# Which engine joins the weight words and subtracts the low parts: attention and two expert layers on one Trainium2 core

## The chip, the cores and the metric

The kernel runs on one core of a Trainium2 chip. Its engines are PE (TensorE, matmuls), DVE (VectorE), ACT (ScalarE), POOL (GpSimd) and SP (SyncE, which here only issues DMAs). Each works through its own list of instructions in order and waits on semaphores for the others. The metric is device microseconds (us) of one execution; lower is better.

## The reference, cut to what matters

```python
# attention with a decaying state; r, k, v, w: (2, 8, 768, 48), u: (8, 48)
for t in range(S):
    cur = einsum('bhd,bhe->bhde', u * k_t, v_t)
    y[:, :, t] = einsum('bhd,bhde->bhe', r_t, state + cur)
    state = w_t[..., None] * state + einsum('bhd,bhe->bhde', k_t, v_t)
x = y as (1536, 384)
h = x @ w_in                       # first layer, (384, 2048), weights in float64
x = (h * sigmoid(h)) @ w_out       # (2048, 384), weights in float64
e = argmax(x @ w_gate)             # second layer: one of 8 experts per token
out = gate_e * (relu(x @ w1[e]) @ w2[e])    # 384 -> 1024 -> 384
```

## The kernel before, in words

**Precision.** Every matmul operand is split in two float32r parts, a high part (a rounding copy on ACT) and a low part (operand minus high part). A product is three matmuls: high·high, high·low, low·high. So each weight piece, each activation tile and each attention output costs one copy and one subtraction on top of the matmuls.

**Weights of the first layer** arrive as float64 words in 16 pieces `rawd` of 128x768 words (`d_load`). A piece becomes float32 in place: `d_s` (lines 344, 345; 342 where the string `L3` says ACT) shifts the low 32-bit word's top three mantissa bits into place and fetches the sign, both on 16-bit quarter words; `d_abs` (349, ACT) rescales the high word; `d_or` (357, DVE) shifts the high word left by three and joins it with the low one. Then `d_h` (361, ACT) makes the high part in `wt` and `d_c` (369, POOL) the low part.

**Attention** takes 128 tokens of one batch per step, 12 steps (`at1` to `at8b`). DVE runs two scans (168, 180) over the decays `w`, multiplies `kh` (215) and, for steps 0, 1 and 2, `rh` (220; POOL from step 3 on). POOL multiplies `tk` (187, 188), DVE reduces it to `dg` (226, one number per head and token), and `at2b` writes `A`, eight 128x128 diagonal matrices with `dg` on the diagonal: ACT and POOL four each for steps 0 and 1 (232, 233), one POOL instruction of 128x1024 from step 2 on (235). DVE copies the masked scores over `A` (268), and PE multiplies.

**The first layer** works in units: 6 chunks of 256 tokens times 8 units of 256 features. `s1` (397) is 18 matmuls into the PSUM tile `s1`, of which there are two; ACT applies Silu twice, to `gh` (403, rounded) and to `sg` in SBUF (404); `s1b` (413) subtracts, `gl = sg - gh`, on DVE in even units and POOL in odd ones; `s2` (422) is 12 matmuls into `acc`. The PSUM tile is free again after the second Silu. Chunk 0 converts the 16 pieces as it goes (`tick`), and the tables `STAGES` and `AHEAD` say in which unit each part of an attention step is issued. After a chunk, `r1` to `r5` route its tokens: 16 products `jk` on DVE (459), some small operations, two indirect DMAs from POOL.

**The second layer** has 32 units of the same form, with Relu (407); its `gl` (415, DVE) reads the PSUM tile itself. The low parts of its weights are on DVE and POOL (384).

**Order.** The first instructions stand in an order written by hand (`manual_schedule`). The rest is ordered by a scheduler from the order of issue, priorities and its own picture of the times, separately for each engine, so an edit in one place can reorder others.

Of the kernel before, what the change touches and what calls it, by code (L numbers as in the profile page):

```python
# [8 lines left out]
F32 = mybir.dt.float32  # L9
# [26 lines left out]

# engine of the third limb subtraction of each weight piece: D = DVE, A = ACT
L3 = "DADADDDDAADDDDAA"
# MoE unit in which each stage of attention steps 2.. is issued
STAGES = (  # L40
# [10 lines left out]
)  # L51
# MoE unit before the loads of steps 3.. are issued
AHEAD = (0, 4, 9, 17, 24, 25, 44, 52, 60)


def bc(ap, shape):
    return ap.to_broadcast(shape)


def fast_path(ctx, tc, wp, rk, tk, vv, uu, ub, wd, wpc, wg, wgb, out, xs, flag):  # L60
# [161 lines left out]
    def at2b(n):  # L222
        d = st[n]
        dg = d["dg"] = wk.tile([128, 8], F32, name="dg")
        if n >= 2:
            nc.vector.tensor_reduce(dg.unsqueeze(2), d["tk"][:, 0].rearrange("p (h d) -> p h d", d=D), AX.X, ALU.add)
        else:
            nc.vector.tensor_copy(dg, d["dp"].rearrange("p a b -> p (a b)"))
        A = d["A"] = wk.tile([128, 8, 128], F32, name="A", bufs=2)
        if n < 2:  # L230
            for h in range(4, 8):
                nc.scalar.activation(out=A[:, h], in_=ident, func=AF.Copy, scale=dg[:, h:h + 1])
            nc.gpsimd.tensor_tensor(out=A[:, 0:4], in0=bc(ident.unsqueeze(1), [128, 4, 128]), in1=bc(dg[:, 0:4].unsqueeze(2), [128, 4, 128]), op=ALU.mult)
        else:
            nc.gpsimd.tensor_tensor(out=A, in0=bc(ident.unsqueeze(1), [128, 8, 128]), in1=bc(dg.unsqueeze(2), [128, 8, 128]), op=ALU.mult)

    def at_q2(n):
        nc.scalar.activation(out=jq, in_=st[n]["QF"], func=AF.Square, accum_out=q2[:, n:n + 1])

# [7 lines left out]
    def at3c(n):  # L247
        nc.scalar.copy(st[n]["Kt"], st[n]["kp"])
# [65 lines left out]
    def at8b(n):  # L314
# [23 lines left out]

    def d_s(m):
        h = dr[m].bitcast(U16).rearrange("p (n t) -> p n t", t=4)  # L340
        if L3[m] == 'A':
            nc.scalar.activation(out=h[:, :, 0], in_=h[:, :, 1], func=AF.Copy, scale=2.0 ** -13, bias=2.0 ** -14 - 0.5)  # L342
        else:
            nc.vector.tensor_scalar(h[:, :, 0], h[:, :, 1], 13, None, op0=ALU.logical_shift_right)  # L344
        nc.vector.tensor_scalar(h[:, :, 1], h[:, :, 3], 1 << 15, None, op0=ALU.bitwise_and)  # L345

    def d_abs(m):
        hi = words(m)[1].bitcast(F32)
        nc.scalar.activation(out=hi, in_=hi, func=AF.Abs, scale=2.0 ** -112)
# [17 lines left out]
    def d_c(m, eng):
        hi = words(m)[1].bitcast(F32)
        lz["pool"] = eng.tensor_tensor(out=wt[m][:, 1], in0=hi, in1=wt[m][:, 0].bitcast(F32), op=ALU.subtract)  # L369
        dr.pop(m)  # L370
# [14 lines left out]

    # ---------------- one pair of feature blocks
    PASS = ((0, 0), (0, 1), (1, 0))
    gt = {}

    def s1(u, w, x, moe1):  # L390
        s = ps.tile([128, 2, 256], F32, name="s1", bufs=2)
        wv = w.rearrange("p l (k f) -> p l k f", k=3)
        for fi in range(2):
            n = 0
            for a, b in PASS:
                for k in range(3):
# [802 lines left out]
```

## Time and profile before

| | us |
|---|---|
| three runs | 507.19, 509.21, 510.77 |
| median | 509.21 |
| profiled execution, first to last instruction | 509.3 |
| chunk 0's result is copied out (line 452, first time) | at 139.5 |
| first matmuls of the second layer | from about 359 |

The page gives no other time for the profiled execution than its span. In the rows below a busy time is the time in which an engine executes; a DVE instruction that has started and is held up counts as busy. `name L123` is the tile and the line. Names have no buffer numbers there.

### The profile page before, as it was taken

The page shows a single profiled execution, that of the slowest core. Times are in us where ns is not written, and L with a number is a line of the kernel's source. Part 1 is how long each engine was busy: PE and PEld are TensorE (multiplying, and loading weights), DVE is VectorE, ACT ScalarE, POOL GpSimd, SP SyncE. Part 2 cuts the span into 40 slices and gives each one's busy share as a digit, 9 for nine tenths or more (in the row PEclk, how much of TensorE's full clock was granted, in tenths as well). Part 3 has the DMA queues.
Part 4 walks back from the last instruction along what each step waited for, and adds up shares of the span by engine and source line. Part 5 has one row for each costly group of instructions (what it writes and reads, how often), then busy time and mean ns, then how long its engine had stood idle before and what let it go on. Part 6 is the DMA issues. An engine that isn't in the chain of part 4 may idle for free.

```text
span 509.3 us, 8293 instructions
## 1 busy us (share of the span) xinstructions
PE 455.6 (89%) x3199; PEld 440.4 (86%) x3199; DVE 343.5 (67%) x616; ACT 217.1 (43%) x384; POOL 249.3 (49%) x208
## 2 busy tenths in 40 slices
PE   6876868785999998899999999689999999999993
PEld 3865768674999998899999999689999999999992
DVE  7999999999697699249679524963665554555220
ACT  3673446355524331322442324253655555664110
POOL 6447576576735751513152234761646655663111
PEclk9667968698799999899999999979999999999997
DMA  8645436434583322102020001175477666651000
GB/s 296 245 124 193 169 130 246 163 147 174 180 276 117 97 75 62 66 1 64 22 97 2 1 31 26 43 274 218 144 261 224 229 218 227 202 194 34 23 28 30
DMA packets 20769, 68.17 MB, mean 134 GB/s; under 512 B 3042, under 2 KB 7293, under 8 KB 20720
## 3 DMA queue, kind: packets, MB, share of 16 engines
q1 hardware_dynamic: 16848, 59.65, 34.7%
q0 software_dynamic: 1792, 4.73, 2.5%
q10 hardware_dynamic: 2080, 3.16, 1.8%
q8 instruction: 27, 0.44, 0.3%
q14 instruction: 22, 0.18, 0.1%
HBM read 59.64 MB, written 8.68 MB: 134 GB/s over the span
## 4 chain that ended last, share of the span: by engine, by line
PE 55%; DVE 26%; issue 11%; ACT 4%; POOL 1%; DMA 1%; SPq 0%; POOLq 0%; DVEq 0%; ACTq 0%
PE s L397 24%; PE acc L422 20%; DVE jk L459 5%; DVE rawd L345 3%; PE y L288 3%; DVE rawd L344 3%; DVE QF L168 3%; PE acc L533 2%; DVE gl L413 2%; DVE QF L180 2%; DVE rawd L357 2%; PE sc L256 1%; ACT rawd L342 1%; PE y L286 1%; DMA rk<-rk 1%
## 5 line engine op out<-in xcount | busy, mean ns | idle before, releaser
L397 PE MATMUL s<-xh,wt 128*128 128x256 f32 x960 | 164.3, 294 | 9.1 <-ACT sg L404 7.3
L422 PE MATMUL acc<-wt,gh 128*128 128x384 f32 x576 | 154.6, 348 | 9.8 <-ACT wt L361 8.1
L397 PEld LDWEIGHTS s<-xh,wt 128*128 128x128 f32 x960 | 140.4, 199 | 11.7 <-ACT sg L404 7.9
L422 PEld LDWEIGHTS acc<-wt,gh 128*128 128x128 f32 x576 | 104.0, 194 | 12.0 <-ACT wt L361 8.9
L422 PE MATMUL acc<-wt,gl 128*128 128x384 f32 x288 | 97.7, 344 | 0.0
L397 PE MATMUL s<-xl,wt 128*128 128x256 f32 x480 | 88.6, 294 | 1.4 <-DVE xl L320 1.4
L384 POOL TENSOR_TENSOR wt<-raw,wt 128x768 fp32r<-128x768 f32 x34 | 64.7, 1908 | 46.6 <-ACT wt L383 46.5
L397 PEld LDWEIGHTS s<-xl,wt 128*128 128x128 f32 x480 | 73.4, 201 | 1.9 <-DVE xl L320 1.7
L383 ACT CAST wt<-raw 128x768 fp32r<-128x768 f32 x64 | 52.8, 834 | 15.6 <-PE acc L422 11.8
L459 DVE SCALAR_TENSOR_TENSOR jk<-xr,wgr 128x384 f32<-128x384 f32 x80 | 57.2, 768 | 0.3
L384 DVE TENSOR_TENSOR wt<-raw,wt 128x768 fp32r<-128x768 f32 x30 | 37.1, 1241 | 29.7 <-ACT wt L383 29.7
L422 PEld LDWEIGHTS acc<-wt,gl 128*128 128x128 f32 x288 | 55.9, 195 | 0.0
L403 ACT ACTIVATE gh<-s 128x512 fp32r<-128x512 f32 x48 | 28.7, 597 | 61.9 <-PE s L397 61.8
L413 POOL TENSOR_TENSOR gl<-sg,gh 128x512 fp32r<-128x512 f32 x24 | 34.4, 1432 | 34.4 <-PE sc L256 18.1
L415 DVE SCALAR_TENSOR_TENSOR gl<-s,gh 128x512 fp32r<-128x512 f32 x32 | 22.1, 691 | 38.9 <-ACT gh L407 38.9
L369 POOL TENSOR_TENSOR wt<-rawd,wt 128x768 fp32r<-128x768 f32 x16 | 34.9, 2185 | 24.4 <-ACT wt L361 24.4
L413 DVE TENSOR_TENSOR gl<-sg,gh 128x512 fp32r<-128x512 f32 x24 | 24.7, 1029 | 27.3 <-ACT sg L404 26.9
L407 ACT ACTIVATE gh<-s 128x512 fp32r<-128x512 f32 x32 | 19.2, 600 | 51.3 <-PE s L397 46.0
L288 PE MATMUL y<-A,vv 128*96 128x128 f32 x192 | 33.6, 308 | 2.7 <-DVE A L268 1.3
L515 POOL DMA_INDIRECT out<-o,er x16 | 19.4, 1209 | 31.9 <-ACT o L644 28.6
L288 PEld LDWEIGHTS y<-A,vv 128*96 128x96 f32 x192 | 27.6, 189 | 4.6 <-DVE A L268 2.7
L404 ACT ACTIVATE sg<-s 128x512 f32<-128x512 f32 x48 | 28.5, 594 | 0.0
(181 smaller groups left out, 633.9 us busy)
## 6 DMA issues: line engine op xcount, KB each, us to landing
raw<-wpc SPq DMA_DIRECT2D x32, 768.0 KB, 5.5
rawd<-wd SPq DMA_DIRECT2D x16, 768.0 KB, 4.9
rk<-rk SPq DMA_DIRECT2D x11, 512.0 KB, 4.5
tk<-tk SPq DMA_DIRECT2D x10, 384.0 KB, 3.3
vv<-vv SPq DMA_DIRECT2D x12, 288.0 KB, 2.8
xs<-fillt ACTq DMA_DIRECT2D x2, 1544.0 KB, 7.6
er<-xs SPq DMA_DIRECT2D x16, 193.0 KB, 2.4
w<-wp SPq DMA_DIRECT2D x11, 259.0 KB, 2.7
```

The lines of the kernel that those rows point to most:

```text
L288: nc.tensor.matmul(o1, d["vv"][:, p, h * 48:h * 48 + 96], d["A"][:, 2 * p + h], start=n < B and h == 0, stop=h == 1)
L369: lz["pool"] = eng.tensor_tensor(out=wt[m][:, 1], in0=hi, in1=wt[m][:, 0].bitcast(F32), op=ALU.subtract)
L383: nc.scalar.copy(t[:, 0], r)
L384: lo.tensor_tensor(out=t[:, 1], in0=r, in1=t[:, 0].bitcast(F32), op=ALU.subtract)
L397: nc.tensor.matmul(s[:, fi], wv[:, a, k, fi * 128:fi * 128 + 128], x[b][:, k], start=n == 0, stop=n == 8)
L403: nc.scalar.activation(out=gh, in_=s, func=AF.Silu)
L404: lz["sg"] = nc.scalar.activation(out=sg, in_=s, func=AF.Silu)
L413: (nc.gpsimd if u % 2 else nc.vector).tensor_tensor(out=gl, in0=s, in1=gh.bitcast(F32), op=ALU.subtract)
L415: nc.vector.scalar_tensor_tensor(out=gl, in0=s, scalar=0.0, in1=gh.bitcast(F32), op0=ALU.max, op1=ALU.subtract)
L422: lz["s2"] = nc.tensor.matmul(acc[j][:, 0:DM], g[a][:, fi, j * 128:j * 128 + 128], w[:, b, fi * DM:fi * DM + DM], start=first and fi == 0 ...
L459: nc.vector.scalar_tensor_tensor(out=jk, in0=ro[c]["xr"][j][:, 0:DM], scalar=1.0, in1=wgr[e // 4][:, e % 4], op0=ALU.mult, op1=ALU.mult, a ...
L515: i = nc.gpsimd.indirect_dma_start(out=dst, out_offset=bass.IndirectOffsetOnAxis(ap=idx, axis=0), in_=src, in_offset=None, bounds_check=bo ...
```

## The change

Five edits; the general path and the second layer keep their code.

1. A piece of weights is joined with 32-bit operations: `d_x` shifts the low word right by 29 in one operation (DVE for even pieces, ACT for odd ones), then one DVE operation with two inputs takes the sign of the high word and joins it with the low one. `d_or` stays. Where 26 16-bit operations stood on DVE (16 of line 345, 10 of line 344), there are 8 32-bit shifts and 16 two-input operations of the form of line 357; ACT has 8 shifts instead of 6.
2. The low part of a piece is on DVE for even pieces and on POOL for odd ones, where all 16 were on POOL.
3. `A` is written by eight ACT instructions of 128x128 in every step.
4. The second Silu writes the PSUM tile in place; `sg` is gone.
5. Every `gl` and every `rh` is on DVE.

```diff
-L3 = "DADADDDDAADDDDAA"
+L3 = "DADADADADADADADA"
+LO = "DPDPDPDPDPDPDPDP"
@@ at2b
-        if n < 2:
-            for h in range(4, 8):
-                nc.scalar.activation(out=A[:, h], in_=ident, func=AF.Copy, scale=dg[:, h:h + 1])
-            nc.gpsimd.tensor_tensor(out=A[:, 0:4], in0=bc(ident...), in1=bc(dg[:, 0:4]...), op=ALU.mult)
-        else:
-            nc.gpsimd.tensor_tensor(out=A, in0=bc(ident...), in1=bc(dg...), op=ALU.mult)
+        for h in range(8):
+            nc.scalar.activation(out=A[:, h], in_=ident, func=AF.Copy, scale=dg[:, h:h + 1])
@@ at_stages
-        at2r(n, nc.vector if n == 2 else nc.gpsimd)
+        at2r(n, nc.vector)
@@ d_s becomes d_x
-            nc.scalar.activation(out=h[:, :, 0], in_=h[:, :, 1], func=AF.Copy, scale=2.0 ** -13, bias=2.0 ** -14 - 0.5)
+            nc.scalar.activation(out=words(m)[0], in_=...bitcast(U16)...[:, :, 1], func=AF.Copy, scale=2.0 ** -13, bias=2.0 ** -14 - 0.5)
         else:
-            nc.vector.tensor_scalar(h[:, :, 0], h[:, :, 1], 13, None, op0=ALU.logical_shift_right)
-        nc.vector.tensor_scalar(h[:, :, 1], h[:, :, 3], 1 << 15, None, op0=ALU.bitwise_and)
+            nc.vector.tensor_scalar(lo, lo, 29, None, op0=ALU.logical_shift_right)
+        nc.vector.scalar_tensor_tensor(out=lo, in0=hi, scalar=1 << 31, in1=lo, op0=ALU.bitwise_and, op1=ALU.bitwise_or)
@@ d_c
-        eng.tensor_tensor(...)               # called with nc.gpsimd
+        eng = nc.gpsimd if LO[m] == "P" else nc.vector
@@ s1, s1b
-            sg = gp.tile([128, 2, 256], F32, name="sg", bufs=2)
             nc.scalar.activation(out=gh, in_=s, func=AF.Silu)
-            nc.scalar.activation(out=sg, in_=s, func=AF.Silu)
+            nc.scalar.activation(out=s, in_=s, func=AF.Silu)
-            (nc.gpsimd if u % 2 else nc.vector).tensor_tensor(out=gl, in0=s, in1=gh..., op=ALU.subtract)
+            nc.vector.tensor_tensor(out=gl, in0=s, in1=gh..., op=ALU.subtract)
```

Two places show how the lists of the engines change. The first is POOL in chunk 0, when steps 2 and 3 of attention are prepared (`tk` is multiplied by POOL, `wt` is a low part of a piece). Before, and then with the change:

```order
L369 TENSOR_TENSOR wt_308<-rawd_146,wt_308 128x768
L235 TENSOR_TENSOR A_426<-ident_90,dg_424 128x1024
L369 TENSOR_TENSOR wt_347<-rawd_148,wt_347 128x768
L369 TENSOR_TENSOR wt_395<-rawd_150,wt_395 128x768
L187 TENSOR_TENSOR tk_509<-tk_509 128x384
L413 TENSOR_TENSOR gl_420<-sg_421,gh_419 128x512
L369 TENSOR_TENSOR wt_442<-rawd_312,wt_442 128x768
L188 TENSOR_TENSOR tk_509<-tk_509,ut_113 128x384
L220 TENSOR_TENSOR rh_635<-rk_483,QF_624 128x512
```

```order
L190 TENSOR_TENSOR tk_519<-tk_519 128x384
L191 TENSOR_TENSOR tk_519<-tk_519,ut_113 128x384
L364 TENSOR_TENSOR wt_314<-rawd_146,wt_314 128x768
L364 TENSOR_TENSOR wt_400<-rawd_150,wt_400 128x768
L190 TENSOR_TENSOR tk_724<-tk_724 128x384
L191 TENSOR_TENSOR tk_724<-tk_724,ut_113 128x384
```

What stays on POOL in chunk 0 is `tk` and every other low part; `A`, `gl` and `rh` have left its list, and `tk` of the next step no longer stands behind them.

The second is ACT at the first unit of the first layer (`gh` and the Silu behind it are unit 0's, `A` is of step 2). Before, and then with the change:

```order
L349 ACTIVATE rawd_150<-rawd_150 128x768
L403 ACTIVATE gh_371<-s1_352 128x512
L404 ACTIVATE sg_373<-s1_352 128x512
L361 CAST wt_308<-rawd_146 128x768
L361 CAST wt_347<-rawd_148 128x768
L361 CAST wt_395<-rawd_150 128x768
```

```order
L348 ACTIVATE rawd_146<-rawd_146 128x768
L234 ACTIVATE A_430<-ident_90,dg_428 128x128 x8
L402 ACTIVATE gh_377<-s1_358 128x512
L403 ACTIVATE s1_358<-s1_358 128x512
L360 CAST wt_314<-rawd_146 128x768
L360 CAST wt_353<-rawd_148 128x768
L360 CAST wt_400<-rawd_150 128x768
```

The eight diagonals, which wait for `dg` from DVE, now stand on ACT's list ahead of unit 0's Silu and of three casts that PE's weights wait for.

## Rows read from the trace of the kernel before

**Rows 1.** The page's first part: busy us (share of the span) xinstructions, by engine.
```profile
PE 455.6 (89%) x3199; PEld 440.4 (86%) x3199; DVE 343.5 (67%) x616; ACT 217.1 (43%) x384; POOL 249.3 (49%) x208
```
**Rows 2.** Stretches: length, busy of PE PEld DVE ACT POOL, granted PE clock, DMA share, GB/s.
```profile
0.00:139.50 139.50, 104.84 (x598) 93.86 (x599) 127.58 (x150) 71.82 (x117) 89.47 (x84) 0.78 0.53 188
139.50:350.00 210.50, 200.65 (x1531) 197.87 (x1530) 145.56 (x355) 72.33 (x151) 89.13 (x78) 0.98 0.26 86
350.00:509.30 159.30, 150.16 (x1074) 148.65 (x1072) 70.38 (x111) 72.92 (x117) 70.70 (x46) 0.98 0.45 149
```
**Rows 3.** Waits of PE up to 350 us: what waited, for whom, us, times, longest.
```profile
PE s L397 <- ACT sg L404: 7.3, 2, 3.7
...
PE cu L483 <- DVE oh L473: 5.9, 1, 5.9
```
**Rows 4.** Timeline of DVE from 38 to 47 us: start, duration, instruction.
```profile
40.38 2.65 DVE L344 TENSOR_SCALAR rawd<-rawd 128x768 uint16<-128x768 uint16 x1
42.83 2.29 DVE L220 TENSOR_TENSOR rh<-rk,QF 128x512 f32<-128x512 f32 x1
```
**Rows 5.** Timeline of POOL over the same stretch.
```profile
39.87 4.71 POOL L369 TENSOR_TENSOR wt<-rawd,wt 128x768 fp32r<-128x768 f32 x2
```
**Rows 6.** Groups of DVE instructions, 0 to 139.5 us: busy us, mean ns, idle before.
```profile
L345 DVE TENSOR_SCALAR rawd<-rawd 128x768 uint16<-128x768 uint16 x16 | 22.9, 1443 | 1.0 <-ACT rawd L342 0.8
L357 DVE SCALAR_TENSOR_TENSOR rawd<-rawd 128x768 int32<-128x768 int32 x16 | 18.7, 1182 | 1.0 <-ACT rawd L349 1.0
L344 DVE TENSOR_SCALAR rawd<-rawd 128x768 uint16<-128x768 uint16 x10 | 18.3, 1830 | 0.0
L168 DVE TENSOR_TENSOR_SCAN QF<-w,lead 128x517 f32<-128x517 f32 x6 | 10.5, 1743 | 1.3 <-DMA w<-wp 1.3
...
L413 DVE TENSOR_TENSOR gl<-sg,gh 128x512 fp32r<-128x512 f32 x5 | 7.3, 1462 | 0.0
```
**Rows 7.** Single lines, whole run: duration ns min/median/max, first and last start.
```profile
L344 DVE TENSOR_SCALAR rawd<-rawd x10: 1009/2041/2750, 17.0 to 107.3; 128x768 uint16<-128x768 uint16 x10
...
L345 DVE TENSOR_SCALAR rawd<-rawd x16: 998/1130/2608, 18.1 to 123.5; 128x768 uint16<-128x768 uint16 x16
...
L357 DVE SCALAR_TENSOR_TENSOR rawd<-rawd x16: 934/957/2679, 20.9 to 127.5; 128x768 int32<-128x768 int32 x16
...
L413 DVE TENSOR_TENSOR gl<-sg,gh x24: 674/692/2372, 38.1 to 344.2; 128x512 fp32r<-128x512 f32 x24
...
L415 DVE SCALAR_TENSOR_TENSOR gl<-s,gh x32: 678/692/693, 363.2 to 494.8; 128x512 fp32r<-128x512 f32 x32
...
L168 DVE TENSOR_TENSOR_SCAN QF<-w,lead x11: 1191/2039/2923, 3.6 to 257.5; 128x517 f32<-128x517 f32 x11
...
L384 DVE TENSOR_TENSOR wt<-raw,wt x30: 944/1115/4234, 339.2 to 466.8; 128x768 fp32r<-128x768 f32 x30
```
**Rows 8.** Groups of POOL instructions, 0 to 139.5 us, as Rows 6.
```profile
L369 POOL TENSOR_TENSOR wt<-rawd,wt 128x768 fp32r<-128x768 f32 x16 | 34.9, 2185 | 24.4 <-ACT wt L361 24.4
L235 POOL TENSOR_TENSOR A<-ident,dg 128x1024 f32<-128x1024 f32 x5 | 12.7, 2540 | 3.3 <-DVE dg L226 3.3
...
L413 POOL TENSOR_TENSOR gl<-sg,gh 128x512 fp32r<-128x512 f32 x5 | 8.9, 1787 | 6.1 <-ACT sg L404 3.7 <-ACT PC L175 2.4
L220 POOL TENSOR_TENSOR rh<-rk,QF 128x512 f32<-128x512 f32 x3 | 4.4, 1459 | 7.2 <-PE y L286 7.2
```
**Rows 9.** Groups of ACT instructions, 0 to 139.5 us, as Rows 6.
```profile
L342 ACT ACTIVATE rawd<-rawd 128x768 uint16<-128x768 uint16 x6 | 11.4, 1953 | 0.0
...
L232 ACT ACTIVATE A<-ident,dg 128x128 f32<-128x128 f32 x8 | 2.6, 391 | 5.6 <-DVE dg L228 5.6
```
**Rows 10.** Timeline of PE at 205 us.
```profile
205.25 0.81 PE L397 MATMUL s<-xh,wt 128*128 128x256 f32 x3 [3.67 <-ACT sg L404]
```
**Rows 11.** Chain that ended last, in the first layer: start, us, what.
```profile
215.72 2.15 PE s L397 x18
217.86 2.09 PE acc L422 x12
```

More of the change, by code (lines that the diff above doesn't have):

```diff
@@ L14 @@
 U16 = mybir.dt.uint16
+U32 = mybir.dt.uint32
 AF = mybir.ActivationFunctionType
@@ L229, in at2b @@
         A = d["A"] = wk.tile([128, 8, 128], F32, name="A", bufs=2)
-        if n < 2:
-            for h in range(4, 8):
-                nc.scalar.activation(out=A[:, h], in_=ident, func=AF.Copy, scale=dg[:, h:h + 1])
-            nc.gpsimd.tensor_tensor(out=A[:, 0:4], in0=bc(ident.unsqueeze(1), [128, 4, 128]), in1=bc(dg[:, 0:4].unsqueeze(2), [128, 4, 128]), op=ALU.mult)
-        else:
-            nc.gpsimd.tensor_tensor(out=A, in0=bc(ident.unsqueeze(1), [128, 8, 128]), in1=bc(dg.unsqueeze(2), [128, 8, 128]), op=ALU.mult)
+        for h in range(8):
+            nc.scalar.activation(out=A[:, h], in_=ident, func=AF.Copy, scale=dg[:, h:h + 1])
     def at_q2(n):
@@ L322, in fast_path @@
     at_stages = [
-        at1, lambda n: (at2k(n), at2r(n, nc.vector if n == 2 else nc.gpsimd), at_q2(n)), at2b, lambda n: (at3(n), at3c(n)), lambda n: (at4(n), at4b(n)), at5,
+        at1, lambda n: (at2k(n), at2r(n, nc.vector), at_q2(n)), at2b, lambda n: (at3(n), at3c(n)), lambda n: (at4(n), at4b(n)), at5,
         lambda n: (at7(n), at6(n, 0)), lambda n: at6(n, 1), lambda n: (at8a(n), at8b(n)),
@@ L337, in words, with d_x, d_t @@
         return v[:, :, 0], v[:, :, 1]
-    def d_s(m):
-        h = dr[m].bitcast(U16).rearrange("p (n t) -> p n t", t=4)
-        if L3[m] == 'A':
-            nc.scalar.activation(out=h[:, :, 0], in_=h[:, :, 1], func=AF.Copy, scale=2.0 ** -13, bias=2.0 ** -14 - 0.5)
-        else:
-            nc.vector.tensor_scalar(h[:, :, 0], h[:, :, 1], 13, None, op0=ALU.logical_shift_right)
-        nc.vector.tensor_scalar(h[:, :, 1], h[:, :, 3], 1 << 15, None, op0=ALU.bitwise_and)
-    def d_abs(m):
+    def d_x(m):
+        lo, hi = (x.bitcast(U32) for x in words(m))
+        if L3[m] == "A":
+            nc.scalar.activation(out=words(m)[0], in_=dr[m].bitcast(U16).rearrange("p (n t) -> p n t", t=4)[:, :, 1], func=AF.Copy, scale=2.0 ** -13, bias=2.0 ** -14 - 0.5)
+        else:
+            nc.vector.tensor_scalar(lo, lo, 29, None, op0=ALU.logical_shift_right)
+        nc.vector.scalar_tensor_tensor(out=lo, in0=hi, scalar=1 << 31, in1=lo, op0=ALU.bitwise_and, op1=ALU.bitwise_or)
+    def d_t(m):
         hi = words(m)[1].bitcast(F32)
@@ L351, in d_a @@
     def d_a(m):
-        d_s(m)
-        d_abs(m)
+        d_x(m)
+        d_t(m)
     def d_or(m):
@@ L361, in d_h, with d_c @@
         lz["act"] = nc.scalar.copy(t[:, 0], words(m)[1].bitcast(F32))
+    def d_c(m):
+        eng = nc.gpsimd if LO[m] == "P" else nc.vector
+        eng.tensor_tensor(out=wt[m][:, 1], in0=words(m)[1].bitcast(F32), in1=wt[m][:, 0].bitcast(F32), op=ALU.subtract)
+        dr.pop(m)
     def d_b(m):
@@ L365, in d_b @@
         d_h(m)
[L367 to L370, printed above, removed]
+        d_c(m)
     raw = {}
@@ L401, in s1 @@
         if moe1:
-            sg = gp.tile([128, 2, 256], F32, name="sg", bufs=2)
             nc.scalar.activation(out=gh, in_=s, func=AF.Silu)
-            lz["sg"] = nc.scalar.activation(out=sg, in_=s, func=AF.Silu)
+            lz["sg"] = nc.scalar.activation(out=s, in_=s, func=AF.Silu)
         else:
-            sg = s
             nc.scalar.activation(out=gh, in_=s, func=AF.Relu)
-        gt[u] = (gh, gl, sg)
+        gt[u] = (gh, gl, s)
     def s1b(u, moe1):
@@ L412, in s1b @@
         if moe1:
-            (nc.gpsimd if u % 2 else nc.vector).tensor_tensor(out=gl, in0=s, in1=gh.bitcast(F32), op=ALU.subtract)
+            nc.vector.tensor_tensor(out=gl, in0=s, in1=gh.bitcast(F32), op=ALU.subtract)
         else:
@@ L691, in tick @@
             d_b(i - 1)
-            d_c(i - 1, nc.gpsimd)
             if i + 3 < N1:
@@ L720, in fast_path @@
         at2b(1)
-        d_s(0)
+        d_x(0)
+        d_t(0)
         at4c(1, 0)
-        d_abs(0)
         at4c(1, 1)
@@ L734, in fast_path @@
         at8b(1)
-        d_s(1)
-        d_abs(1)
-        d_c(0, nc.gpsimd)
+        d_a(1)
+        d_c(0)
         d_or(1)
         d_h(1)
-        d_c(1, nc.gpsimd)
+        d_c(1)
     ticks[0] = 2
```

## The prediction

> **What bounds the kernel now.** The page's first part gives PE 89% of the span [rows 1], which hides where the time is open. The busy times by stretch divide it [rows 2]. Up to 139.5 us (**stage A**, until chunk 0's result is copied out) DVE is busy for 127.6 us while PE has 104.8 us of work at a granted clock of 0.78: DVE sets the pace. From there to 350 us (**stage B**, chunks 1 to 5) PE is busy for 200.65 of 210.5 us at 0.98: PE sets it, and only its waits are to be had, two of which make nearly all of them, 3.7 us on ACT's second Silu and 5.9 us on the routing's last DVE result [rows 3, 10]. From 350 us on (second layer) PE works without a break but at the tail, and the change touches nothing there.
>
> Then look at why DVE is so busy in stage A. The timeline shows one shift taking 2.65 us and one product 2.29 us while POOL runs two low parts [rows 4, 5]; the shortest of the same shift took 1.01 us [rows 7]. A DVE instruction that reads SBUF is held while POOL computes. The held time can be read off as mean minus minimum, times count [rows 6, 7]: L345 16 x 0.445 = 7.1, L357 16 x 0.248 = 4.0, L344 10 x 0.821 = 8.2, L413 5 x 0.788 = 3.9, L168 6 x 0.552 = 3.3, together 26.5 us. One group is never held: line 415, the second layer's subtraction whose first input is in PSUM, took 0.678 to 0.693 us in all 32 cases, though POOL works on low parts then too; the first layer's, from SBUF, took up to 2.372 [rows 7].
>
> **What a microsecond of POOL costs DVE.** POOL was busy for 89.5 us in stage A [rows 2]. The five groups give 26.5 / 89.5 = 0.30 us per us, a floor, since other products and the second scan are held too (the 2.29 us one [rows 4]). The ceiling is 1: where both have work they take turns [rows 4, 5]. I take 0.45, near the floor, because the floor covers the largest groups.
>
> **Stage A, taken away.** POOL loses half of its low parts (34.9 / 2 = 17.5 us), `A` (12.7), `gl` (8.9) and `rh` (4.4) [rows 8]: 43.5 us. At 0.45 that gives DVE back 19.6 us (13 at the floor, 26 at 0.6).
>
> **Stage A, added to DVE**, unheld prices. The 26 16-bit operations become 8 shifts and 16 joins: 26 x 1.0 = 26.0 us against 8 x 1.0 + 16 x 0.934 = 22.9, so -3.1 [rows 7]. The 32-bit shift does not occur before; its bounds are 0.5 us (half of the 16-bit one) and 1.0 (the same), and I take 1.0, the nearest row. Low parts: 8 x 0.944 (line 384 on DVE) = +7.6; at that line's median, 1.115, 8.9 [rows 7]. Five more `gl` (10 against 5 by the order of the lists): at line 415's 0.692, +3.5. Three `rh` at line 413's 0.674, the same size: +2.0. Together **+10.0 us**. Net for DVE: -19.6 + 10.0 = **-9.6 us**, with bounds -3 and -16. DVE idles for only 12 us of stage A, so the stage follows: I count -10.
>
> [...] The joins read and write every other 32-bit word, as line 357 does, whose 16 cases start at 0.934 us for 768 words [rows 7]. [...]
>
> **ACT.** In stage A it gets 48 more diagonals (7 steps of 8 against 8 in all) at 2.6 / 8 = 0.325 us = 15.6, and two more shifts at 1.95 = 3.9 [rows 9]: 71.8 + 19.5 = 91 us of some 130 [rows 2]. That is covered as long as ACT is not late: it is 70% busy, DVE over 90%. The first block of diagonals stands ahead of unit 0's Silu and three casts and waits for `dg`; DVE itself is behind there, so I cost it at nothing, and if the cover is gone it is 8 x 0.325 = 2.6 us a block. Its two fill DMAs are in no hurry. On SP the same loads are issued; on POOL the scatters stand behind less.
>
> **Silu in place** costs ACT nothing: the Silu from PSUM to SBUF and the one beside it are one form, and I know no row of ACT writing PSUM; bounds are -0.1 and +0.6 us each (free of the held time, or a second pass), and both lie under PE. But the PSUM tile is now held until `gl`. In stage B a tile's turn is: the unit's s, then acc 2.09, s 2.15, acc 2.09 until the next use [rows 11], 6.3 us, less two Silus of 0.6 and a `gl` of 0.69: 4.4 us of slack for DVE's queue.
>
> **Stage B.** The 3.67 us wait [rows 10] ends on ACT's Silu, which stood behind operations that waited for DVE's routing products and scan, held by POOL's `A`, `gl` and `rh`. These go; DVE gets one `rh` and one more `gl` (1.4 us) in that chain. I take -4, clock recovery included (bounds 0 and -6). The 5.9 us wait stays: POOL's low parts of the second layer hold that chain. For new short waits on `gl` +1 (0 to +4).
>
> **Sum** against the profiled execution: 509.3 - 10 - 4 + 1 = **496 us**. Its span equals the median of the three runs (509.21) within 0.1, so nothing is shifted. Own bounds: 509.3 - 16 - 6 = 487 and 509.3 - 3 + 0 = 506.
>
> **The rivals.**
> - *The hand-overs set stage A, not DVE's load* (0.20). Each piece goes DVE, ACT, DVE, ACT, then to its low part; with ACT at 70% and DVE with a new wait for ACT's cast in eight low parts, DVE's savings turn into idle time. For it: ACT's list now has diagonals that wait for DVE ahead of casts. Against it: DVE idled little before. Stage A -3 at most, stage B -4 to +1: 502 to 510, say 507.
> - *Slower: the held PSUM tile* (0.18). In stage B a `gl` stands behind seven or eight routing products of 384 columns, 8 x 0.55 = 4.4 us (0.55 is an estimate between line 413's 0.674 for 512 columns and three quarters of it [rows 7]), or behind a block of diagonals (2.6 us) on ACT ahead of its Silus. When both meet, 7.0 us stand against 4.4 of slack, and PE waits for 2.6 us and runs at the lower clock after it. With two such meetings in each of five chunks, 10 x 2.6 = 26, less 10 for stage A and 4 saved nowhere: 509.3 - 10 + 26 = 525 at worst, half of it, 512, at best; I take 519. It decides from the point where DVE's queue ahead of a `gl` exceeds 4.4 us. Against it: the second layer runs with the same hold and PE never pauses.
> - *More relief* (0.10). If POOL's remaining 46 us hold DVE as little as 0.2 us per us and the shift is at 0.5 us, stage A drops by 22 and stage B by 6: 482. For it: `gl` leaves the held kind altogether.
> - That the change doesn't move what it says is excluded by the order of the lists.
>
> **Chances and range.** The forecast has 0.52. For this kernel 1% is 5 us, about what the three runs differ by. Faster by over 1% (below 504): forecast nearly whole, more relief, a little of the hand-overs: 0.62. Within 1%: 0.20. Slower: 0.18. The range from 482 to 514 takes the forecast (0.52), the hand-overs (0.20), half of more relief and the lower edge of the slower rival: 0.8.
>
> **What the profile of the changed kernel would show.** Right: chunk 0 copied out near 129 us; POOL busy there 45 us or less; DVE 115 to 120; the DVE subtraction `gl` at 0.7 us without long cases; joins with a minimum of 0.93; PE's wait at some 200 us gone, the one before the last routing still there; the second layer as long as now. [...] The forecast fails first if held time per us of POOL stays above 0.6 for what remains, since then half of the relief is gone.

## The result, and the profile after

The changed kernel takes 487.35 us (median of 4 runs, 485.73 to 489.42) against 508.88 us: the ratio is 0.958, with a 95% interval from 0.954 to 0.962. The forecast was faster, 496 us, range 482 to 514: the sign and the range held, the gain was 21.5 us instead of 13.

First the page's first part, after (columns as in [rows 1]).

```profile
PE 444.0 (92%) x3199; PEld 429.8 (89%) x3199; DVE 322.1 (66%) x655; ACT 239.0 (49%) x474; POOL 154.0 (32%) x155
```

POOL lost 95 us of work, ACT took 22 more, and DVE, which was given work, is busy for 21 us less. Of the 24.2 us between the two profiled executions, PE's idle time makes 12.6 (53.7 to 41.1); the other 11.6 are the same 3199 products in less time, at a mean granted clock of 0.945 of full speed instead of 0.923.

Now the stretches of the changed kernel (columns as in [rows 2]): to chunk 0's copy, to chunk 4's copy, the rest.

```profile
0.00:124.90 124.90, 96.85 (x612) 87.30 (x613) 113.14 (x165) 81.53 (x168) 43.71 (x63) 0.82 0.63 214
124.90:292.40 167.50, 167.50 (x1283) 164.72 (x1282) 112.63 (x321) 69.51 (x166) 21.49 (x34) 1.00 0.21 67
292.40:485.10 192.70, 179.65 (x1308) 177.78 (x1307) 96.27 (x170) 87.94 (x142) 88.84 (x59) 0.98 0.46 157
```

The same cuts in the kernel before, of which the first is in [rows 2]:

```profile
139.50:313.70 174.20, 170.22 (x1297) 167.55 (x1296) 117.03 (x299) 57.61 (x127) 66.41 (x62) 0.99 0.21 67
313.70:509.30 195.60, 180.59 (x1308) 178.97 (x1307) 98.91 (x167) 87.64 (x142) 93.42 (x63) 0.97 0.46 154
```

Chunk 0 is out 14.6 us earlier, chunks 1 to 4 take 6.7 us less, the rest 2.9 less: 24.2 us between the two profiled executions (485.1 against 509.3). In the middle stretch PE now never pauses: 167.50 of 167.50 us at a clock of 1.00.

DVE's groups up to chunk 0's copy in the changed kernel (columns as in [rows 6]); line 344 is the join, 343 the shift, 364 the low part.

```profile
L356 DVE SCALAR_TENSOR_TENSOR rawd<-rawd 128x768 int32<-128x768 int32 x16 | 17.5, 1098 | 0.1
L344 DVE SCALAR_TENSOR_TENSOR rawd<-rawd 128x768 uint32<-128x768 uint32 x16 | 17.3, 1080 | 0.3 <-ACT rawd L341 0.2
L364 DVE TENSOR_TENSOR wt<-rawd,wt 128x768 fp32r<-128x768 f32 x8 | 10.3, 1290 | 0.0
L171 DVE TENSOR_TENSOR_SCAN QF<-w,lead 128x517 f32<-128x517 f32 x6 | 8.2, 1369 | 1.3 <-DMA w<-wp 1.3
L411 DVE TENSOR_TENSOR gl<-s,gh 128x512 fp32r<-128x512 f32 x10 | 6.8, 685 | 2.3 <-ACT s L403 2.2
...
L343 DVE TENSOR_SCALAR rawd<-rawd 128x768 uint32<-128x768 uint32 x8 | 4.4, 546 | 0.0
```

The means have come down to 1.1 us for the joins and 1.4 for the scan (1.74 in [rows 6]). `gl`, one of whose operands is in PSUM, takes 0.685 us and is never held (at most 0.693 in all 48 cases of the run). The shift takes 0.546, half of the shortest 16-bit one, 1.009 [rows 7].

How one instruction is held is seen at 98 us: the timeline of DVE, and of POOL, in the changed kernel.

```profile
97.16 0.96 DVE L344 SCALAR_TENSOR_TENSOR rawd<-rawd 128x768 uint32<-128x768 uint32 x1 [0.18 <-ACT rawd L341]
98.04 2.38 DVE L223 TENSOR_TENSOR rh<-rk,QF 128x512 f32<-128x512 f32 x1
100.34 0.55 DVE L343 TENSOR_SCALAR rawd<-rawd 128x768 uint32<-128x768 uint32 x1
```
```profile
98.00 1.87 POOL L364 TENSOR_TENSOR wt<-rawd,wt 128x768 fp32r<-128x768 f32 x1 [7.50 <-ACT wt L360]
```

POOL's low part ends at 99.87. `rh` began at 98.04 and ended at 100.42, 0.55 us after it: it waited for the rest of POOL's instruction and then ran (its shortest time is 0.68 us). This is no single case. Worked out from all 14 traces: 708 DVE instructions took over 0.1 us longer than the quickest tenth of their form, and 705 of them end 0.09 to 0.15 us less than that quick time after the end of a POOL instruction. So a POOL instruction costs a DVE instruction that it holds what is left of it when that one comes up.

Which instructions are held is narrower than "reads SBUF". Those with two operands in SBUF are (the join takes 0.946 to 2.232 us in the changed kernel), and so are the 16-bit shifts with one (1.009 to 2.750 [rows 7]); `gl` with its operand in PSUM isn't (0.665 to 0.693 in the changed kernel), and neither is the sum of `tk` into `dg`, which reads SBUF alone: of its 17 cases in the 14 traces that began beside POOL's work none was held. Its ten cases in the kernel before:

```profile
L226 DVE TENSOR_REDUCE dg<-tk x10: 527/546/573, 35.0 to 242.5; 128x8 f32<-128x384 f32 x10
```

POOL can be held as well when DVE comes first. The first product of `tk`, in the changed kernel (columns as in [rows 7]), takes 1.0 us and up to 1.9, the latter at 44.09 us, where a scan on DVE had begun at 43.55 and ended 0.8 us before the product did:

```profile
L190 POOL TENSOR_TENSOR tk<-tk x10: 1008/1096/1937, 21.2 to 183.5; 128x384 f32<-128x384 f32 x10
```

So POOL's busy time has held time in it too.

Last, the waits of PE in the changed kernel (columns as in [rows 3]).

```profile
PE s L397 <- DVE gl L411: 5.1, 2, 2.7
...
PE cu L481 <- DVE oh L471: 0.3, 1, 0.3
```

The 3.67 us on ACT's Silu and the 5.87 on `oh` [rows 3, 10] are gone, and in their place stand two waits for the PSUM tile that `gl` keeps, 2.4 us at 53 us and 2.7 us at 308 us.

### The profile page after: what moved, and what is told of

It reads as the page before. It is cut to its first block, busy times and chain, and to the rows that moved or that the text cites. A ratio compares the mean times of both kernels' runs of the same rounds, so it can differ in the third digit from the quotient of the medians.

```text
span 485.1 us, 8394 instructions
## 1 busy us (share of the span) xinstructions
PE 444.0 (92%) x3199; PEld 429.8 (89%) x3199; DVE 322.1 (66%) x655; ACT 239.0 (49%) x474; POOL 154.0 (32%) x155
## 4 chain that ended last, share of the span: by engine, by line
PE 68%; DVE 16%; issue 9%; DMA 2%; POOL 2%; ACT 1%; SPq 0%; POOLq 0%; DVEq 0%
PE s L397 27%; PE acc L420 25%; PE y L287 5%; DVE jk L457 3%; PE sc L255 3%; PE acc L531 2%; DVE rawd L356 2%; DVE rawd L344 2%; PE y L285 2%; DVE QF L171 1%; DVE wt L364 1%; PE U L276 1%; DVE A L267 1%; DMA rk<-rk 1%; POOL out L513 1%
## 5 line engine op out<-in xcount | busy, mean ns | idle before, releaser
L397 PE MATMUL s<-xh,wt 128*128 128x256 f32 x960 | 161.8, 291 | 10.6 <-DVE gl L411 5.1
L420 PE MATMUL acc<-wt,gh 128*128 128x384 f32 x576 | 150.6, 342 | 3.2 <-ACT wt L360 3.2
L397 PEld LDWEIGHTS s<-xh,wt 128*128 128x128 f32 x960 | 138.1, 195 | 12.7 <-DVE gl L411 5.5
L420 PEld LDWEIGHTS acc<-wt,gh 128*128 128x128 f32 x576 | 101.6, 190 | 4.4 <-ACT wt L360 3.7
L411 DVE TENSOR_TENSOR gl<-s,gh 128x512 fp32r<-128x512 f32 x48 | 33.0, 688 | 42.6 <-ACT s L403 41.8
L383 ACT CAST wt<-raw 128x768 fp32r<-128x768 f32 x64 | 52.6, 833 | 14.8 <-PE acc L420 11.9
L384 DVE TENSOR_TENSOR wt<-raw,wt 128x768 fp32r<-128x768 f32 x30 | 34.4, 1154 | 26.0 <-ACT wt L383 25.8
L457 DVE SCALAR_TENSOR_TENSOR jk<-xr,wgr 128x384 f32<-128x384 f32 x80 | 48.6, 660 | 0.2
L405 ACT ACTIVATE gh<-s 128x512 fp32r<-128x512 f32 x32 | 19.2, 600 | 51.2 <-PE s L397 46.0
L234 ACT ACTIVATE A<-ident,dg 128x128 f32<-128x128 f32 x96 | 29.8, 390 | 10.9 <-DVE dg L231 4.6
L190 POOL TENSOR_TENSOR tk<-tk 128x384 f32<-128x384 f32 x10 | 12.5, 1254 | 69.0 <-DMA tk<-tk 53.6
L364 POOL TENSOR_TENSOR wt<-rawd,wt 128x768 fp32r<-128x768 f32 x8 | 16.2, 2034 | 41.9 <-ACT wt L360 41.9
```

Source lines behind the costliest of these rows:

```text
L364: eng.tensor_tensor(out=wt[m][:, 1], in0=words(m)[1].bitcast(F32), in1=wt[m][:, 0].bitcast(F32), op=ALU.subtract)
L383: nc.scalar.copy(t[:, 0], r)
L384: lo.tensor_tensor(out=t[:, 1], in0=r, in1=t[:, 0].bitcast(F32), op=ALU.subtract)
L411: nc.vector.tensor_tensor(out=gl, in0=s, in1=gh.bitcast(F32), op=ALU.subtract)
L420: lz["s2"] = nc.tensor.matmul(acc[j][:, 0:DM], g[a][:, fi, j * 128:j * 128 + 128], w[:, b, fi * DM:fi * DM + DM], start=first and fi == 0 ...
L457: nc.vector.scalar_tensor_tensor(out=jk, in0=ro[c]["xr"][j][:, 0:DM], scalar=1.0, in1=wgr[e // 4][:, e % 4], op0=ALU.mult, op1=ALU.mult, a ...
```

## The experiments

Each variant was timed five or six times beside the kernel before, and its ratio is to those runs; the first two rows are the four runs each of the result. "A" is the time at which chunk 0 is copied out, "A+B" that of chunk 4; DVE and POOL are busy times up to A. "Held" is worked out from the traces: over DVE's instructions up to A, each one's time beyond that which the quickest fifth of its form takes in all runs. It is good to about 2 us: that much it moves with how the quickest cases are chosen. Of the 4.1 us that v_empty keeps, 2.0 are two instructions beside POOL's first products, and the rest is scatter.

| kernel | us | ratio, 95% interval | A | A+B | DVE | POOL | held |
|---|---|---|---|---|---|---|---|
| before | 508.88 | 1 | 139.5 | 313.7 | 127.6 | 89.5 | 39.1 |
| changed | 487.35 | 0.958 (0.954 to 0.962) | 124.9 | 292.4 | 113.1 | 43.7 | 18.6 |
| u_join16 | 490.53 | 0.963 (0.960 to 0.966) | 127.9 | 296.4 | 118.6 | 42.8 | 18.2 |
| u_sgbuf | 489.90 | 0.963 (0.959 to 0.966) | 121.3 | 292.1 | 113.3 | 50.1 | 18.6 |
| u_gl | 487.45 | 0.957 (0.953 to 0.960) | 127.8 | 291.3 | 120.3 | 60.9 | 23.5 |
| u_A | 496.24 | 0.975 (0.972 to 0.979) | 126.5 | 300.0 | 120.5 | 60.1 | 27.7 |
| u_low | 493.44 | 0.969 (0.966 to 0.971) | 130.7 | 298.7 | 117.6 | 62.9 | 29.9 |
| u_rh | 491.75 | 0.965 (0.962 to 0.968) | 128.6 | 299.7 | 115.2 | 48.4 | 22.2 |
| x_tk2 | 487.76 | 0.956 (0.954 to 0.959) | 125.4 | 292.4 | 112.6 | 54.4 | 17.9 |
| v_empty | 483.24 | 0.947 (0.945 to 0.950) | 123.3 | 289.6 | 116.1 | 8.5 | 4.1 |
| v_last | 478.72 | 0.941 (0.938 to 0.943) | 122.6 | 289.6 | 115.8 | 8.5 | 3.7 |
| v_shA | 484.56 | 0.953 (0.950 to 0.956) | 121.9 | 290.3 | 107.8 | 8.5 | 3.4 |
| b_A | 498.51 | 0.978 (0.976 to 0.980) | 133.0 | 303.5 | 123.0 | 77.1 | 34.3 |
| b_gl | 500.86 | 0.982 (0.979 to 0.984) | 131.2 | 306.3 | 125.9 | 83.1 | 34.2 |

Held time follows POOL's busy time over the whole table: from 4.1 at 8.5 to 39.1 at 89.5 is 0.43 us per us, and that line gives every kernel within 3.5 us but x_tk2. "A" doesn't stand for the same work everywhere: PE has run 576 (u_sgbuf) to 650 (u_gl) products by then, 598 in the kernel before and 612 in the changed one. A+B does, with 1893 to 1901.

**One part undone.** u_join16:

```diff
-            nc.scalar.activation(out=words(m)[0], in_=..., func=AF.Copy, ...)
+            nc.scalar.activation(out=h[:, :, 0], in_=h[:, :, 1], func=AF.Copy, ...)
-            nc.vector.tensor_scalar(lo, lo, 29, None, op0=ALU.logical_shift_right)
-        nc.vector.scalar_tensor_tensor(out=lo, in0=hi, scalar=1 << 31, in1=lo, op0=ALU.bitwise_and, op1=ALU.bitwise_or)
+            nc.vector.tensor_scalar(h[:, :, 0], h[:, :, 1], 13, None, op0=ALU.logical_shift_right)
+        nc.vector.tensor_scalar(h[:, :, 1], h[:, :, 3], 1 << 15, None, op0=ALU.bitwise_and)
```

> The changed kernel with only the join of a piece back in 16-bit operations (8 shifts and 16 signs of the form of line 345 of the kernel before on DVE; ACT's 8 shifts in 16 bit). Load theory (stage A follows DVE's busy time with its held time): 8 shifts at 1.0 for 0.55 us are +3.6, 16 signs at 1.0 for 0.95 are +0.8, and more held time, 24 operations by up to 0.3 us = up to 7: chunk 0 copied out at 129 to 136 instead of 124.9 us, time 492 to 498 instead of 487.4. Hand-over theory (the order and the waits set the stage, not DVE's load): chunk 0 within 1.5 us of 124.9, time within 1.5 us of 487.

It took 490.5 us, 3 more than the changed kernel, with A 3 us later: the direction of the load theory at less than its lower end, and above the 488.5 of the other. The two intervals overlap, so the 3 us are not clear of noise. DVE's two groups in this kernel up to A, and the shift in the whole run:

```profile
L344 DVE TENSOR_SCALAR rawd<-rawd 128x768 uint16<-128x768 uint16 x16 | 18.7, 1178 | 0.5 <-ACT rawd L341 0.4
...
L343 DVE TENSOR_SCALAR rawd<-rawd 128x768 uint16<-128x768 uint16 x8 | 9.6, 1201 | 0.0
```
```profile
L343 DVE TENSOR_SCALAR rawd<-rawd x8: 1006/1031/2400, 17.0 to 106.1; 128x768 uint16<-128x768 uint16 x8
```

18.7 + 9.6 = 28.3 us against 17.3 + 4.4 = 21.7: 6.6 us more in these two groups, most of it the shift (9.6 against 4.4). Held time as a whole did not rise (18.2 against 18.6), which was the term that I had too large. ACT's eight shifts went back to 16 bits as well and take 15.5 us instead of 7.3, so the run does not show DVE's part alone.

u_sgbuf and u_gl:

```diff
+            sg = gp.tile([128, 2, 256], F32, name="sg", bufs=2)
-            nc.scalar.activation(out=s, in_=s, func=AF.Silu)
+            nc.scalar.activation(out=sg, in_=s, func=AF.Silu)
# u_gl, besides:
-            nc.vector.tensor_tensor(out=gl, ...)
+            (nc.gpsimd if u % 2 else nc.vector).tensor_tensor(out=gl, ...)
```

> The changed kernel with only the second Silu back in an SBUF tile of its own; every gl stays on DVE, but reads two SBUF tiles. Load theory: 11 gl of stage A are held again, about 0.4 us each = +4 us there, and the two waits of PE for s on gl (2.4 and 2.7 us) go: 485 to 490, chunk 0 at 125 to 129. If the held PSUM tile were the larger cost: both waits gone, chunk 0 at 122 to 124, time 481 to 484.

> The changed kernel with gl as before: second Silu in SBUF, every other gl on POOL. Load theory: POOL +7.5 us in stage A, which hold DVE by 3.4 at 0.45, six gl left on DVE held by about 0.4 each = +2.4, five gl gone from DVE = -3.4: +2 in stage A, and a wait on POOL's gl or on ACT behind the routing in the second half of the first layer: 488 to 493. If gl's engine does not matter: 486 to 488.

u_sgbuf took 489.9 us, u_gl 487.5; both intervals overlap that of the changed kernel, so neither can be told from it. In u_sgbuf chunk 0 is out at 121.3 us, where the load theory had 125 to 129, but with 36 products fewer done, and A+B is the same (292.1 against 292.4). The waits for `gl` are gone, but PE waits 4.3 us for a low part on POOL and 4.2 us for `oh`. Its `gl`, and that of b_gl (below), which reads PSUM, up to A:

```profile
L413 DVE TENSOR_TENSOR gl<-sg,gh 128x512 fp32r<-128x512 f32 x10 | 8.9, 890 | 0.4 <-ACT sg L404 0.4
```
```profile
L413 DVE TENSOR_TENSOR gl<-s,gh 128x512 fp32r<-128x512 f32 x10 | 6.9, 688 | 0.2
```

The operand in PSUM saves 0.2 us of held time for each `gl` there. In u_gl the 5.9 us wait for `oh` is back where the changed kernel has 3.0 us of waits, and A+B is 1.1 us shorter: the two nearly cancel (its profiled execution is 1.5 us longer). My lower end for u_gl, 488, was missed by half a microsecond; the other case, that `gl`'s engine does not matter once the other parts are in, held, although DVE is busy for 7.2 us more up to A.

u_A, u_low and u_rh put `A`, the low parts and `rh` back:

```diff
# u_A
-        for h in range(8):
-            nc.scalar.activation(out=A[:, h], in_=ident, func=AF.Copy, scale=dg[:, h:h + 1])
+            nc.gpsimd.tensor_tensor(out=A, ...)        # and half of it where n < 2, as before
# u_low
-LO = "DPDPDPDPDPDPDPDP"
+LO = "PPPPPPPPPPPPPPPP"
# u_rh
-at2r(n, nc.vector)
+at2r(n, nc.vector if n == 2 else nc.gpsimd)
```

> The changed kernel with only A as before (POOL multiplies, half of it on ACT in steps 0 and 1). Load theory: POOL +12.7 us in stage A at 0.45 holds DVE by 5.7 us more: chunk 0 at 129 to 132, time 491 to 495. Hand-over theory (ACT's diagonals stand ahead of Silu and casts and cost): chunk 0 at 121 to 125, time 483 to 487.

> The changed kernel with only the low parts of the first layer's pieces all on POOL again. Load theory: DVE loses 8 low parts at 0.95 = -7.6 us, POOL gains 8 at 2.0 = 16, which hold DVE by 7.3 at 0.45: nothing net, 486 to 490 (487.4 for the changed kernel). Hand-over theory: PE's weights come later behind POOL's queue, waits of PE on POOL's wt appear, 491 to 496.

> The changed kernel with only rh back on POOL (DVE keeps it in steps 0 to 2). Load theory: four rh of stage A leave DVE (-2.8 us unheld), POOL gets four of 1.46 = 5.8 us and holds DVE by 2.6 to 3.2: nothing net, 486 to 489. If the wait of PE for sc on rh decides, which POOL computes in 1.5 us instead of 0.7 and behind its own list: 489 to 493.

u_A: 496.2 us, 8.9 more. The hand-over theory (A on ACT costs) is out. But it does not come where I put it: A is only 1.6 us later, and the next stretch is 6.0 longer. PE had done 31 products fewer at A and does them in that stretch (1314 against 1283), which makes 4.3 of the 6.0 us. That stretch (columns as in [rows 2]), and PE's waits for `gl` in this kernel:

```profile
126.50:300.00 173.50, 171.78 (x1314) 168.51 (x1314) 120.52 (x326) 57.95 (x127) 31.17 (x39) 1.00 0.21 66
```
```profile
PE s L401 <- DVE gl L415: 9.4, 4, 3.9
```

With POOL loaded again `gl` comes late, and PE waits for the tile, for 5.1 of these 9.4 us before A.

u_low: 493.4 us, 6.1 more, in the range of the hand-over theory. Two things add up: POOL's 19.2 us more hold DVE by 11.3, more than the 7.6 that it loses (DVE is busy for 4.5 us more), and PE waits on POOL's low parts as well as on `gl`:

```profile
PE s L397 <- DVE gl L411: 7.6, 3, 4.5
PE acc L420 <- POOL wt L364: 4.8, 2, 3.3
```

u_rh: 491.8 us, 4.4 more, again the waits' range and not the load's; held time is up by 3.6, and PE waits for `gl` 6.6 us and once 5.4 us for a low part on DVE. The wait for `rh` itself, which I had named, is only 2.0, less than the 4.2 of the changed kernel; so the range was met for another reason.

**One part alone**, on the kernel before. b_A has the change's `A` and b_gl its second Silu in place with every `gl` on DVE; the diffs are those of u_A and u_gl the other way round.

> The kernel before with A alone changed (eight ACT diagonals in every step). Load theory: POOL -12.7 us in stage A gives DVE back 5.7, and ACT is released earlier in the second half of the first layer (-2 to -4): 499 to 504 against 509.3. If A pays only together with the in-place Silu, by the waits on gl: 506 to 510.

> The kernel before with the second Silu in place and every gl on DVE, and nothing else of the change. Load theory: five gl of stage A leave POOL (8.9 us, 4.0 of held time at 0.45), those on DVE are no longer held (-3.9), five more at 0.69 are +3.5: -4 us there, 503 to 507 against 509.3. Held tile (the prediction's slower rival): with POOL's A, rh and low parts still holding DVE, gl comes late and PE waits for s on gl several times, up to 10 us in all: 509 to 516.

b_A: 498.5 us, half a microsecond below the load theory's range; A comes 6.5 us earlier. b_gl: 500.9 us, below both ranges. Its waits of PE:

```profile
PE s L397 <- DVE gl L413: 7.3, 5, 2.7
```

The held tile costs what the slower rival said by kind, five waits, and the kernel is 9.1 us faster all the same. DVE's busy time in stage A falls by just 1.7 us, so load is not most of this gain. Its idle time falls from 11.9 to 5.3, and the longest wait of the kernel before in that stage is gone, that for POOL's `tk`, which stood behind a `gl` on POOL's list:

```profile
DVE dg L226 <- POOL tk L188: 4.0, 1, 4.0
```

That this wait paid is not shown: it ended at 138 us, while PE had work. PE's share of b_gl's page says where the gain appears:

```profile
PE 446.0 (89%) x3199; PEld 431.4 (86%) x3199; DVE 341.8 (68%) x640; ACT 217.4 (43%) x384; POOL 213.9 (43%) x184
```

PE idles for 53.7 us of the 499.7, as long as before, and does the same products in 9.6 us less, at a granted clock of 0.943 instead of 0.923. What in the new order gives PE the higher clock stays open.

Alone the two parts bring 11.2 and 9.1 us (medians of the same rounds), together nearly the whole 21.5; undone from the whole, one costs 8.9 and the other nothing. The parts are not additive.

**More POOL work, and none.** x_tk2 repeats POOL's product of `tk` with `ut` (which changes the diagonals, so only its time counts; that it changes nothing, as the expectation says, is not so). v_empty puts `tk` and all low parts of the first layer on DVE; v_last the second layer's first low parts too (eight: on POOL there are 26 left of 34; the expectation says six); v_shA is v_empty with every shift on ACT.

```diff
# x_tk2: this line twice
         nc.gpsimd.tensor_tensor(out=t[:, 0], in0=t[:, 0], in1=ut, op=ALU.mult)
# v_empty
-LO = "DPDPDPDPDPDPDPDP"
+LO = "DDDDDDDDDDDDDDDD"
-        nc.gpsimd.tensor_tensor(out=t[:, 0], ...)      # both products of tk
+        nc.vector.tensor_tensor(out=t[:, 0], ...)
# v_last, besides
-                ensure(2 * i + 1, nc.gpsimd)
+                ensure(2 * i + 1)
# v_shA: v_empty with
-L3 = "DADADADADADADADA"
+L3 = "AAAAAAAAAAAAAAAA"
```

> The changed kernel with POOL's multiplication of tk by the mask done twice (the second changes nothing). POOL gets 7 operations of 1.4 us = 9.7 us more in stage A and 3 later, DVE nothing. Load theory at 0.45: DVE is held by 4.4 us more, time 490 to 493. If DVE's idle time (11.8 us of stage A) takes it up: 486 to 489.

> The changed kernel with tk and all low parts of the first layer on DVE too, so that POOL does next to nothing in stage A. Load theory: DVE gets 14 tk at 0.52 = 7.3 us and 8 low parts at 0.95 = 7.6 us, and gives back the rest of its held time, some 20 us: -5 us, 480 to 484. Hand-over theory: a longer list on DVE with more waits for ACT's casts in it and POOL's parallel work lost: 488 to 496.

> v_empty with the second layer's first six low parts on DVE too, which POOL computes while DVE has the last routing's products. Load theory: five products held by 1.6 us each run free, the wait of PE on gl at 305 us (2.7 us) goes, DVE gets 6 x 0.95 us: 479 to 482 against 483.2 for v_empty. Rival: the six low parts stand in DVE's list ahead of the routing and delay it as much: 483 to 487.

> v_empty with the shift of every piece on ACT (eight more there). Load theory: DVE loses 8 x 0.55 = 4.4 us of stage A, in which it is now busy for 116 of 123 us and never held: 479 to 482 against 483.2. Hand-over theory: ACT gets 8 x 0.92 = 7.4 us more, each ahead of a join that DVE then waits for: 483 to 488.

x_tk2: 487.8 us, the same. POOL has 10.7 us more and DVE is held no longer (17.9 against 18.6). So 0.43 is an average over what stands beside POOL's work, not a law for each instruction. The traces show why the sum stayed: the products of `tk` do hold DVE more, 8.4 us in 14 cases against 6.0 in 8, but the low parts, which now come at other moments, hold it less, 5.8 us in 4 cases against 8.9 in 7. And some 3.6 of POOL's 10.7 us are POOL itself being held (estimated like DVE's held time). That DVE's idle time takes it up, as the second case had it, is not what happened; that another order would leave it as cheap is not shown.

v_empty: 483.2 us, in the load theory's range, and clear of the changed kernel. Its DVE groups up to A:

```profile
L356 DVE SCALAR_TENSOR_TENSOR rawd<-rawd 128x768 int32<-128x768 int32 x16 | 15.2, 949 | 0.8 <-ACT rawd L348 0.7
L344 DVE SCALAR_TENSOR_TENSOR rawd<-rawd 128x768 uint32<-128x768 uint32 x16 | 15.1, 951 | 0.2
L364 DVE TENSOR_TENSOR wt<-rawd,wt 128x768 fp32r<-128x768 f32 x16 | 15.1, 949 | 0.2 <-ACT wt L360 0.2
L171 DVE TENSOR_TENSOR_SCAN QF<-w,lead 128x517 f32<-128x517 f32 x7 | 8.6, 1232 | 1.4 <-DMA w<-wp 1.4
```

With POOL nearly silent every group runs close to its shortest: 0.949, 0.951 and 0.949 us where the changed kernel has 1.098, 1.080 and 1.290. With the ends counted above, this shows that POOL, and not the form or the data, makes DVE's long cases.

v_last: 478.7 us, lower than both theories had it and the fastest of all, 1.8% below the changed kernel. The same piece of the last routing, in the changed kernel on DVE and on POOL, and in v_last on DVE:

```profile
296.91 2.19 DVE L457 SCALAR_TENSOR_TENSOR jk<-xr,wgr 128x384 f32<-128x384 f32 x1
...
301.16 2.20 DVE L457 SCALAR_TENSOR_TENSOR jk<-xr,wgr 128x384 f32<-128x384 f32 x1
...
303.29 2.19 DVE L457 SCALAR_TENSOR_TENSOR jk<-xr,wgr 128x384 f32<-128x384 f32 x1
```
```profile
296.56 8.51 POOL L384 TENSOR_TENSOR wt<-raw,wt 128x768 fp32r<-128x768 f32 x4 [2.38 <-ACT wt L383]
```
```profile
293.08 0.55 DVE L457 SCALAR_TENSOR_TENSOR jk<-xr,wgr 128x384 f32<-128x384 f32 x1
...
294.04 0.95 DVE L384 TENSOR_TENSOR wt<-raw,wt 128x768 fp32r<-128x768 f32 x1
...
294.91 0.55 DVE L457 SCALAR_TENSOR_TENSOR jk<-xr,wgr 128x384 f32<-128x384 f32 x1
```

One low part on DVE takes 0.95 us. On POOL it takes 1.85 and holds one routing product by 1.6 us. PE has neither the wait for `gl` nor that for `oh` in v_last's last routing, and what follows chunk 4's copy is 187.7 us long, against 192.7 in the changed kernel. The routing's `oh` starts only 0.4 us sooner after that copy (17.1 against 17.5 us); what no longer keeps PE is the `gl` between its products.

v_shA: 484.6 us, slower than v_empty; the hand-over theory holds. The stretch up to A (columns as in [rows 2]) in v_empty, then in v_shA:

```profile
0.00:123.30 123.30, 98.41 (x624) 88.66 (x626) 116.05 (x197) 84.97 (x181) 8.45 (x41) 0.81 0.64 219
```
```profile
0.00:121.90 121.90, 94.88 (x605) 84.25 (x605) 107.78 (x179) 87.58 (x175) 8.46 (x41) 0.83 0.65 219
```

DVE is busy for 8.3 us less up to A (8 shifts left its list, and 10 other instructions now come after A), and A comes 1.4 us earlier: the rest became idle time (14.1 against 7.2 us). Of the 16 joins only the first waits for ACT's shift, 3.3 us at 20 us; the theory had it of each. The larger part is that `gl` now waits for the second Silu, which it does not in v_empty (DVE's waits up to A in v_shA):

```profile
DVE gl L411 <- ACT s L403: 4.8, 2, 2.4
```

So taking more load from DVE at that point no longer makes the kernel faster.

## Why the prediction was right, and where it was short

- **POOL's price for DVE, 0.45 us per us: right.** POOL lost 45.8 us in stage A (forecast 43.5) and held time fell by 20.5 (forecast 19.6). The rows told the mechanism, by the `gl` that is never held beside the one that is [rows 7], and a floor of 0.30; the step from there to 0.45 was a choice, and that it met the size is luck. "A DVE instruction that reads SBUF is held" was too wide (the sum into `dg` above).
- **What DVE is given, +10.0 us: too dear.** Its unheld time rose by 6.6 (113.7 - 18.6 against 127.6 - 39.1, both with overlaps of records taken out). The term that failed is "8 x 1.0 for the 32-bit shift": it takes 0.546 us, near the lower of my two bounds, and 8 x 0.45 is 3.6. The 0.546 us are about half of the 16-bit shift's 1.03 (median in u_join16). The 16 joins were counted at 0.934 us, the shortest case of the same form in the kernel before [rows 7], and start at 0.946 (median 0.955).
- **Stage A, -10: it was -14.6**, which is DVE's busy time (127.6 to 113.1, -14.5). DVE's idle time stayed at 12 us, which fits a stage set by its load. The single undos say that load is not the whole: DVE's busy time up to A rises by 7.4 us in u_A, 4.5 in u_low, 2.1 in u_rh and 7.2 in u_gl, and the kernels lose 8.9, 6.1, 4.4 and 0.1 us.
- **Stage B, -4: it was -6.7** to chunk 4's copy. PE's idle time there went from 4.0 us to none, which is the -4. The other 2.7 us are PE's busy time (170.2 to 167.5): 14 fewer products, done in stage A now, and a clock of 1.00 for 0.99. The cause that was named for the 3.67 us wait fits b_A, where it is gone with `A` alone off POOL. The clock as a whole was left out of the sum: PE is busy for 11.6 us less over the run, with a granted clock of 0.82 for 0.78 in stage A. What a wait costs beside itself is seen in the kernel before. Behind the 3.67 us wait PE is busy without a break from 207 to 209 us at 0.52, and from 209 to 211 at 1.00; the traces of both kernels show no level but 0.50 and 1.00. Behind the 5.9 us wait that ends at 332.9 us PE is busy without a break at 0.50:

```profile
334.00:336.00 2.00, 2.00 (x11) 2.00 (x11) 1.12 (x6) 0.09 (x1) 0.56 (x1) 0.50 1.04 433
```

- **The 5.9 us wait "stays": wrong.** It became 2.7 on `gl` and 0.3 on `oh`. The cause that I named for it, POOL's low parts of the second layer, is right (v_last takes it away). But the order is such that PE now waits for the PSUM tile ahead of `oh`, and the routing is 1.5 us shorter.
- **The slower rival**: its mechanism is there, in the changed kernel twice (2.4 and 2.7 us), in b_gl five times, in u_A for 9.4 us. Its size was wrong: no wait repeats in every chunk, not even in b_gl, where POOL holds DVE nearly as much as before (34.2 us of 39.1). What the tile costs and what the PSUM operand saves cancel (u_sgbuf can't be told from the changed kernel).
- **ACT's bill, 15.6 + 3.9 us, at nothing**: right, though the bill itself was half that. The diagonals came to 14.8 us more, but the shifts, which write 32-bit words now, to 4.1 less (7.3 against 11.4 [rows 9]). ACT is busy for 81.5 of 124.9 us. The Silu that writes PSUM takes no longer than the one to SBUF (0.592 us at the median in both kernels); the bounds of -0.1 and +0.6 us that I gave it were estimates, and no run shows either.

What stays open is how the 21.5 us divide among the parts: alone and undone they give different shares, and no run separates order, load and PE's clock inside one part.

## What to carry to other kernels

When one engine's work holds up another's, the price of work on the slower one is its time and what it holds up on the other. Read it as the difference between the mean and the shortest case of the same instruction, and compare with a form that is never held; here a low part on POOL cost 1.85 us and in the last routing held DVE by another 1.6, where DVE alone needed 0.95. Before taking all of it away, look at whether the faster engine still sets the stage: v_last gained 8.6 us more by taking `tk` and low parts off POOL, while eight shifts fewer on DVE (v_shA) gained nothing.

## What was not expected of the hardware

- A shift of every other 32-bit word in place takes 0.546 us for 768 words (mean, changed kernel), the 16-bit one in the same pieces 1.03 (median, u_join16), and ACT's shift takes 0.917 us when it writes 32-bit words, 1.953 when it writes 16-bit ones [rows 9]:

```profile
L341 ACT ACTIVATE rawd<-rawd 128x768 int32<-128x768 uint16 x8 | 7.3, 917 | 1.0 <-DMA rawd<-wd 0.9
```

- A held DVE instruction waits for the end of POOL's instruction and not only for its share of turns (705 of 708 held instructions in the 14 traces; 2.38 us for one that takes 0.69, beside a POOL instruction of 1.87 that began 0.04 us earlier).
- 10.7 us more of POOL's busy time left DVE's held time as it was (x_tk2): the repeated products held DVE, and the low parts held it less.
